# Fused chunk attention and FFN: transposed scores straight into PV, 128-token attention units between FFN steps, q and k loaded in runs of four tokens

## The chip, the cores and the metric

One core of one Trainium2 chip. The time is the device time of one execution in microseconds (us), the median of several runs; lower is better. A profile (a trace of every instruction on every engine) of one execution goes with each kernel. The span in a profile is about 2 us shorter than the timed execution, so I compare spans with spans and times with times. The span of the kernel before, 337.1 us, happens to equal its median time: by the same 2 us its profiled execution took about 339 us (an estimate; that execution is not among the four timed ones).

The engines are named as in the profile: PE is TensorE (matmul), PEld its weight loads, DVE is VectorE, ACT is ScalarE, POOL is GpSimd, which here issues the loads, and SP issues the stores.

## The reference

```python
# attention: q, k, v are (8 batches, 8 heads, 576 tokens, 64), cut into chunks of 64 tokens
scores = 1/sqrt(64) * q_c @ k_c.T        # 64 x 64 per chunk and head
attn   = softmax(scores)
out    = attn @ v_c
# heads side by side: x is (4608 tokens, 512); FFN:
a = x @ w1;  b = x @ w2                  # 512 -> 1024
y = ((a * b) @ w3) @ w_out               # 1024 -> 1024 -> 512
```

Both kernels compute w3 @ w_out once ("the w3 product", 1024 x 512), work in bf16, and run the FFN on nine tiles of 512 tokens: per tile 64 matmuls for a and b and 32 for the output, each with 512 columns. An attention chunk is 64 x 64 x 64: the profile lists its score matmuls as 64\*64 with 64 columns, those of the FFN as 128\*128 with 512.

## The kernel before

Per batch and pair of heads, it transposes q and k on TensorE, computes scores with the query on the partitions, normalises on VectorE, transposes the attention weights on TensorE, and multiplies them with v (this product is called PV). Two FFN steps are let through after each head pair.

```python
for hp in range(NHP):                                   # pairs of heads
    for c in range(NCH):                                # 9 chunks
        nc.tensor.transpose(qT_ps[:, c, :], q_bs[:, c, h0*D:(h0+2)*D], ident64)
        nc.tensor.transpose(kT_ps[:, c, :], k_bs[:, c, h0*D:(h0+2)*D], ident64b)
    nc.scalar.copy(qT[:], qT_ps[:]);  nc.scalar.copy(kT[:], kT_ps[:])
    ...                                                 # scores: lhsT = qT, rhs = kT
    nc.scalar.activation(attn_unn[...], sc_ps[...], Exp, scale=scale, bias=0.0)
    nc.vector.reduce_sum(ssum[:], attn_unn[:], axis=X)
    nc.vector.reciprocal(srec[:, :, 0], ssum[:, :, 0])
    nc.vector.tensor_mul(attn_n[:], attn_unn[:], srec.to_broadcast([P, NCH, CHUNK]))
    ...
        nc.tensor.transpose(aT_ps[:, cc, :], attn_n[:, c0 + cc, :], ident)
    nc.vector.tensor_copy(attnT[...], aT_ps[...])
    ...                                                 # PV: lhsT = v, rhs = attnT
    nc.vector.tensor_copy(xt[:, hp, ...], vo_ps[...])
    pump_moe(PUMP_RATE)
```

(cut: the loads, the w3 product, the FFN steps). All loads go through one queue; q and k come as rows of one token and head.

The softmax here doesn't subtract the row's maximum and nothing guards it: scores larger than these inputs give would overflow.

## Time and profile before

The time is 337.1 us (median of 4 runs, 336.4 to 340.9).

| reading | value | view |
|---|---|---|
| span | 337.1 us | page |
| PE busy | 303.4 us, 90% | page |
| DVE, ACT busy | 165.6, 130.3 us | page |
| one batch of 576 tokens in the steady part | 31.75 us, that is 7.06 us per 128 tokens | chain of waits |
| steady part without any attention | 5.18 us per 128 tokens (24 matmuls of 512 columns at 216 ns) | timeline |

The page of the kernel before: the busy line, and two rows of the span cut into 40 slices of 8.4 us (busy share in tenths; PEclk is the granted TensorE clock in tenths):

```profile
PE 303.4 (90%) x3008; PEld 147.7 (44%) x3008; DVE 165.6 (49%) x360; ACT 130.3 (39%) x245; POOL 111.9 (33%) x146
...
PE   1317999889999999999999999999999999999995
...
PEclk9999999759999999999999999999999999999999
```

PE is nearly idle for three slices, and in the eighth and ninth slices the clock is down. After that everything looks full. Busy time by stretch, for the stretch after the start (columns: busy us and count for PE, PEld, DVE, ACT, POOL, then clock, DMA share, GB/s):

```profile
core 0: us, PE busy (x) PEld busy (x) DVE busy (x) ACT busy (x) POOL busy (x), PEclk, DMA share, GB/s
80.80:333.20 252.40, 248.59 (x2487) 117.34 (x2485) 136.05 (x260) 108.19 (x205) 61.44 (x77) 1.00 0.64 71
```

Of 252.4 us, PE is busy 248.6: the steady part is bound by PE's own work. From 80 to 290 us PE waited for another engine 2.3 us in all (us in total, times, longest):

```profile
PE vo_ps L226 <- DVE attnT L218: 2.3, 11, 0.2
```

The chain of waits (start us, length us, what) shows the wait at the start and one period of the steady part:

```profile
9.25 18.12 DMA tile_bf<-in_moe_w_out_dram
...
184.40 1.40 PE o_ps L125 x6
186.86 0.77 DVE ssum L206
187.90 0.77 DVE attn_n L210
...
216.15 1.40 PE o_ps L125 x6
```

The 18.1 us are the load of w_out, on which the w3 product waits. The same o_ps step recurs after 31.75 us. The row sum and the product of the softmax, 0.77 us each, stand in the chain one after the other.

The groups that the change touches (line, engine, operation, tile written and read, shapes, count; busy us and mean ns; idle time before them and who ended it):

```profile
L216 PE MATMUL aT_ps<-ident,attn_n 128*64 128x128 bf16 x288 | 29.4, 230 | 4.4 <-DVE attn_n L210 2.9
L187 ACT COPY qT<-qT_ps 128x576 bf16<-128x576 bf16 x32 | 20.5, 639 | 21.3 <-PE kT_ps L184 17.6
...
L226 PE MATMUL vo_ps<-attnT,v_bs 64*64 64x64 bf16 x576 | 21.5, 199 | 3.6 <-DVE attnT L218 3.6
```

### The profile page before, as it was taken

To read this page: it belongs to the slowest core of one execution; us is meant where nothing else is said; L and a number is where in the kernel's file an instruction comes from. 1 tells how busy PE (TensorE), PEld (TensorE's weight loads), DVE (VectorE), ACT (ScalarE), POOL (GpSimd) and SP (SyncE) were. 2 spreads that over 40 slices of the span, in tenths; PEclk is the share of its full clock that TensorE was granted. 3 is DMA by queue.
4 is the path that set the end of the run, shared out by engine and by line. 5 is a ranking of instruction groups with operands and counts; after the bars stand their busy time and mean duration, and the time that the engine had idled before them with its cause. 6 is when DMAs were issued, how large, how long until landed. Compare 5 with 4: busy or idle time off the path is not lost.

```text
span 337.1 us, 7133 instructions
## 1 busy us (share of the span) xinstructions
PE 303.4 (90%) x3008; PEld 147.7 (44%) x3008; DVE 165.6 (49%) x360; ACT 130.3 (39%) x245; POOL 111.9 (33%) x146
## 2 busy tenths in 40 slices
PE   1317999889999999999999999999999999999995
PEld 0203455554444444444444444444444444444442
DVE  0211346565756555664556465566555664541330
ACT  2201323433334445345543544444445345333332
POOL 8707259848202009502930491078000000000000
PEclk9999999759999999999999999999999999999999
DMA  9999999949729009942990599099902001101103
GB/s 61 163 203 143 207 155 110 135 27 151 50 93 101 4 31 158 122 31 71 155 112 2 90 166 84 2 138 128 73 31 95 2 2 62 64 3 62 62 0 126
DMA packets 121119, 29.30 MB, mean 87 GB/s; under 512 B 113408, under 2 KB 114432, under 8 KB 121088
## 3 DMA queue, kind: packets, MB, share of 16 engines
q0 software_dynamic: 115904, 19.41, 75.0%
q1 hardware_dynamic: 5184, 9.44, 7.5%
q8 instruction: 24, 0.39, 0.5%
q14 instruction: 7, 0.06, 0.1%
HBM read 38.80 MB, written 9.44 MB: 143 GB/s over the span
## 4 chain that ended last, share of the span: by engine, by line
PE 68%; DVE 14%; DMA 5%; ACT 5%; issue 3%; POOL 2%; POOLq 0%; ACTq 0%
PE b_ps L110 16%; PE a_ps L103 15%; PE o_ps L125 11%; PE aT_ps L216 8%; DMA tile_bf<-in_moe_w_out_dram 5%; PE wp L83 5%; PE vo_ps L226 5%; DVE attn_n L210 5%; DVE ssum L206 5%; PE sc_ps L199 3%; ACT attn_unn L202 3%; DVE attnT L218 2%; PE qT_ps L183 2%; PE tp L79 2%; DVE abT L118 1%
## 5 line engine op out<-in xcount | busy, mean ns | idle before, releaser
L103 PE MATMUL a_ps<-xt,tile_bf 128*128 128x512 bf16 x288 | 82.5, 388 | 0.0
L110 PE MATMUL b_ps<-xt,tile_bf 128*128 128x512 bf16 x288 | 81.7, 386 | 0.0
L166 POOL DMA_DIRECT2D qk_bs<-in_q_dram x64 | 51.3, 802 | 82.9 <-PE kT_ps L184 76.6
L117 ACT COPY a_sb<-a_ps 128x512 f32<-128x512 f32 x72 | 42.3, 588 | 84.7 <-PE a_ps L103 84.7
L125 PE MATMUL o_ps<-w3out_sb,abT 128*128 128x512 bf16 x288 | 68.7, 380 | 0.0
L118 DVE TENSOR_TENSOR abT<-a_sb,b_ps 128x512 bf16<-128x512 f32 x72 | 49.2, 683 | 37.3 <-PE b_ps L110 36.4
L168 POOL DMA_DIRECT2D qk_bs<-in_k_dram x64 | 51.3, 802 | 15.0 <-DMA tile_bf<-in_moe_w_dram 11.9
L206 DVE TENSOR_REDUCE ssum<-attn_unn 128x9 f32<-128x576 bf16 x32 | 24.1, 754 | 51.8 <-ACT attn_unn L202 51.8
L228 DVE CAST xt<-vo_ps 128x320 bf16<-128x320 f32 x64 | 29.3, 458 | 30.9 <-PE vo_ps L226 30.0
L103 PEld LDWEIGHTS <-tile_bf 128*128 128x128 bf16 x288 | 26.7, 99 | 28.7 <-issue 1.9
L110 PEld LDWEIGHTS <-tile_bf 128*128 128x128 bf16 x288 | 26.6, 99 | 27.2 <-issue 1.6
L125 PEld LDWEIGHTS <-abT 128*128 128x128 bf16 x288 | 25.2, 98 | 27.5
L202 ACT ACTIVATE attn_unn<-sc_ps 128x320 bf16<-128x320 f32 x64 | 24.7, 410 | 27.8 <-PE sc_ps L199 23.0
L218 DVE COPY attnT<-aT_ps 64x640 bf16<-64x640 bf16 x64 | 28.5, 445 | 11.4 <-PE aT_ps L216 11.2
L132 ACT COPY o_sb<-o_ps 128x512 f32<-128x512 f32 x36 | 21.1, 586 | 31.9 <-PE o_ps L125 31.9
L216 PE MATMUL aT_ps<-ident,attn_n 128*64 128x128 bf16 x288 | 29.4, 230 | 4.4 <-DVE attn_n L210 2.9
L187 ACT COPY qT<-qT_ps 128x576 bf16<-128x576 bf16 x32 | 20.5, 639 | 21.3 <-PE kT_ps L184 17.6
L216 PEld LDWEIGHTS <-attn_n 128*64 128x64 bf16 x288 | 18.4, 112 | 17.4 <-DVE attn_n L210 15.3
L226 PEld LDWEIGHTS <-v_bs 64*64 64x64 bf16 x576 | 14.7, 109 | 25.1 <-issue 16.8
L80 DVE COPY w3Tk<-tp 128x128 bf16<-128x128 bf16 x64 | 11.0, 219 | 28.4 <-PE tp L79 27.6
L226 PE MATMUL vo_ps<-attnT,v_bs 64*64 64x64 bf16 x576 | 21.5, 199 | 3.6 <-DVE attnT L218 3.6
L210 DVE TENSOR_TENSOR attn_n<-attn_unn,srec 128x576 bf16<-128x576 bf16 x32 | 24.3, 758 | 1.1
(23 smaller groups left out, 185.0 us busy)
## 6 DMA issues: line engine op xcount, KB each, us to landing
out_dram<-o_sb SPq DMA_DIRECT2D x36, 256.0 KB, 2.0
qk_bs<-in_q_dram POOLq DMA_DIRECT2D x64, 72.0 KB, 3.9
qk_bs<-in_k_dram POOLq DMA_DIRECT2D x64, 72.0 KB, 3.8
v_bs<-in_v_dram POOLq DMA_DIRECT2D x8, 576.0 KB, 7.6
tile_bf<-in_moe_w_dram POOLq DMA_DIRECT2D x1, 2048.0 KB, 13.7
tile_bf<-in_moe_w_dram POOLq DMA_DIRECT2D x2, 1024.0 KB, 13.4
tile_bf<-in_moe_w_out_dram POOLq DMA_DIRECT2D x1, 1024.0 KB, 18.1
```

The source lines that it names most:

```text
L103: nc.tensor.matmul(a_ps[:], lhsT=w1_sb[:, ki, j * P:(j + 1) * P], rhs=x_slice[:, ki, :], start=(ki == 0), stop=(ki == D_MO - 1),)
L110: nc.tensor.matmul(b_ps[:], lhsT=w2_sb[:, ki, j * P:(j + 1) * P], rhs=x_slice[:, ki, :], start=(ki == 0), stop=(ki == D_MO - 1),)
L117: nc.scalar.copy(a_sb[:], a_ps[:])
L118: nc.vector.tensor_mul(abT[:, j, :], a_sb[:], b_ps[:])
L125: nc.tensor.matmul(o_ps[:], lhsT=abT[:, ki, tk * P:(tk + 1) * P], rhs=w3out_sb[:, ki, :], start=(ki == 0), stop=(ki == D_FO - 1),)
L166: nc.gpsimd.dma_start(q_bs[:, :, h * D:(h + 1) * D], q[b, h].rearrange("(c p) d -> p c d", p=CHUNK))
L168: nc.gpsimd.dma_start(k_bs[:, :, h * D:(h + 1) * D], k[b, h].rearrange("(c p) d -> p c d", p=CHUNK))
L206: nc.vector.reduce_sum(ssum[:], attn_unn[:], axis=mybir.AxisListType.X)
L210: nc.vector.tensor_mul(attn_n[:], attn_unn[:], srec.to_broadcast([P, NCH, CHUNK]))
L216: nc.tensor.transpose(aT_ps[:, cc, :], attn_n[:, c0 + cc, :], ident)
L218: nc.vector.tensor_copy(attnT[:, :nc_, :], aT_ps[:, :nc_, :])
L226: nc.tensor.matmul(vo_ps[ph:ph + CHUNK, cc, :], v_bs[:, j, :], attnT[:, cc, ph:ph + CHUNK], start=True, stop=True)
```

## The change

The intent is to take work off PE, DVE and ACT in the attention and to feed PE in one planned order.

- Scores are computed transposed (key on the partitions), so exp's result is directly the stationary operand of PV: no transpose of the weights. The row sum comes from a column of ones next to v, and division happens after PV.
- The unit of work is 128 tokens with all 8 heads, slotted at fixed places between FFN steps; TensorE keeps the order in which the program was written.
- q and k are loaded in runs of four tokens, so that a descriptor carries four rows of 64. Token 4s+r of a group then lies on partition s in run r, so each transpose yields tokens of one r, and k and the exponentials have to be put back in token order when they are copied out of PSUM.
- w1 and w2 are loaded before w_out and w3.

The core of the diff (cut: renamed constants, the FFN steps, which stay the same, and most of the schedule):

```diff
-            nc.scalar.copy(qT[:], qT_ps[:])
-            nc.scalar.copy(kT[:], kT_ps[:])
+        qp = ps.tile([P, NHP, GCH, RUN, SUB], bf, tag="tr", bufs=2, name="qp")
+        kp = ps.tile([P, NHP, GCH, RUN, SUB], bf, tag="tr", bufs=2, name="kp")
+        for hp in range(NHP):
+            for r in range(RUN):
+                for hh in range(2):
+                    for dst, p0 in ((qp, 0), (kp, CH)):
+                        tr(dst[hh * CH:(hh + 1) * CH, hp, :, r, :],
+                           qk[p0:p0 + GP, hp + hh * NHP, g, r * D:(r + 1) * D],
+                           ident[p0:p0 + GP, p0:p0 + GP])
+        nc.vector.tensor_copy(qT_t[b][:, g].rearrange("p n c t -> p (n c t)"),
+                              qp[:].rearrange("p n c r s -> p (n c r s)"))
+        nc.vector.tensor_copy(
+            kT_t[b][:, g].rearrange("p n c (s r) -> p (n c) r s", r=RUN),
+            kp[:].rearrange("p n c r s -> p (n c) r s"))
...
-            nc.vector.reduce_sum(ssum[:], attn_unn[:], axis=mybir.AxisListType.X)
-            nc.vector.tensor_mul(attn_n[:], attn_unn[:], srec.to_broadcast(...))
-                    nc.tensor.transpose(aT_ps[:, cc, :], attn_n[:, c0 + cc, :], ident)
+        nc.scalar.activation(
+            e[:].rearrange("p n c (s r) -> p (n c) r s", r=RUN),
+            sp[:].rearrange("p n c (r s) -> p (n c) r s", r=RUN),
+            Exp, scale=scale, bias=0.0)
...
+                    mm(xp[ci * CH:(ci + 1) * CH, hh, hp * W:(hp + 1) * W],
+                       lhsT=e[h, hp, ci, :], rhs=v_t[b][h, hp, c, 0:W],   # W = 65
+                       start=True, stop=True)
+        nc.vector.reciprocal(rc[:], xv[:, :, :, D:D + 1])
+        nc.vector.tensor_mul(xn[...], xv[:, :, :, 0:D], rc.to_broadcast(...))
+            tr(tp[:, hp, :], xn[:, hp], ident[:])
+        nc.vector.tensor_copy(xt[:, :, u * UT:(u + 1) * UT], tp[:])
...
+    for i, f in enumerate(fill):         # fill: the FFN steps in order
+        if i in slots:
+            u = slots[i]
+            if u == UPT:                 # the first unit after the start
+                run_T(groups_for(u + 1))
+                do_S(u)
+            slot_a(u)                    # q,k transposes ahead, scores u+1, PV u
+            pending = u
+        f()                              # one FFN step
+        if pending is not None:
+            do_XT(pending)               # output transposes of u
+            pending = None
```

## The prediction

Its sum comes to 284 us.

> **What bounds the kernel now.** TensorE, in two parts. From 80.8 to 333.2 us (busy time by stretch) it is busy 248.6 of 252.4 us at clock 1.00, and waits for another engine only 2.3 us (the waits). A 512-column FFN matmul is issued every 216 ns (timeline), so a 512-token FFN tile costs 96 x 0.216 = 20.7 us, nine tiles 187 us, the w3·w_out product about 17.6 us. One batch of 576 tokens repeats every 31.75 us (chain, 184.40 to 216.15); 23.3 us of it is FFN, so attention costs 8.4 us per batch, 67 us in all. These sum to 272 us. The other 65 us are mostly before 81 us: TensorE is mostly idle to 27 us, waiting for w3 and w_out (chain: 18.1 us on w_out), then attention's vector chain (sum, reciprocal, product, 1.9 us) leaves gaps, and from 64 to 77 us the granted clock is 0.50. [...]
>
> **What changes, with durations from this trace.** Spacings: q/k transposes one pair per 29 ns (two row groups side by side), scores 15 to 16 ns each, PV 27 ns (one row group), a 128-column transpose about 68 ns; a change between 64-wide and 128-wide use about 0.1 us (first qT step 0.13 us, then 0.03)[...].
> - Removed: 288 attention transposes (20 us), their evictions, row sum (24.1 us) and product (24.3 us) on VectorE, q/k evictions on ScalarE (41 us; VectorE takes them).
> - PV alternates row groups: about 16 ns x 576, saves 6 us.
> - Added: q/k transposes 576 to 1536 with 48 columns, about 12 ns each: 8.5 to 18 us; 144 output transposes, 9 us.
> - Per 128-token unit: transposes 0.55, scores 0.26, PV 0.28, output transposes 0.24, mode changes 0.23: 1.55 us against 1.87. For 32 units inside the FFN 50 us against 60.
> - VectorE per unit 3.8 us of 7, ScalarE 2.4: no limit. The output transpose waits one FFN step (1.73 us) for q/k copies, reciprocal and product (2 to 2.4 us): up to 0.4 us stall in some units.
> - DMA: q,k descriptors carry four times as much; w1,w2 come before w_out,w3, so FFN tile 0 starts while w3 lands. At the rates here (150 to 200 GB/s in slices 2 to 6) batch 0 is there at 14 us, the first halves of w1,w2 at 20, w3 at 43, batch 1's q,k at 48 to 50. The in-order PE needs batch 1 inside the w3 product, near 46 us: a 2 to 5 us gap.
>
> **Sum.** FFN start 20 + FFN 187 + w3 product 17.6 + units 50 + gap and slow clock at the start 5 + tail 4 (333.3 to 337.1 here) = 284 us. Of the gain about 40 of 53 us is the start-up, 10 the steady state.
>
> **What would show it.** First FFN matmul near 20 us; TensorE dense from there, with one gap near 46 to 50 us on batch 1's loads; a tile period of 26.5 to 27.5 us; 64 q/k transposes in 0.7 to 1 us; PV at 16 ns; clock 0.5 only before 40 us; VectorE near 45%; packets about half.
>
> **What would make it wrong.** Transposes into strided 16-element runs issued at 25 ns or more (+20 us); [...] stalls at each output transpose turning the clock down; a throttle. Or the transposes overlap in four quadrants and the stalls vanish (-10 us).

## The result

The changed kernel takes 309.1 us (median of 4 runs, 307.5 to 311.2) and is correct. Its ratio to the kernel before is 0.915 (95% interval 0.909 to 0.922). Ratios here are the mean time of one kernel's fast runs over that of the other's of the same rounds, so they are not quite the ratios of the medians that I quote. So it is 8% faster, but 25 us slower than predicted.

The page after:

```profile
PE 258.6 (84%) x3824; PEld 132.4 (43%) x3824; DVE 149.7 (49%) x239; ACT 110.8 (36%) x153; POOL 43.2 (14%) x55
...
PE   1244999679888888988988889889889889999994
...
PEclk9999999959999999999999999999999999999999
```

The start is shorter, but the row that was full of nines is now a pattern of eights and nines. The stretch of FFN tiles with attention between them, after:

```profile
core 0: us, PE busy (x) PEld busy (x) DVE busy (x) ACT busy (x) POOL busy (x), PEclk, DMA share, GB/s
88.17:282.00 193.83, 178.26 (x2657) 88.80 (x2657) 106.41 (x174) 79.32 (x112) 15.82 (x16) 1.00 0.59 72
```

PE is busy 178 of 194 us: it waits here, which it did not before. The groups that answer to those shown of before (tiles: qp and kp hold the q and k transposes in PSUM, qT and kT their copies, sp the scores, e the exponentials, xp the result of PV, xn that result divided by the row sum, tp the output transposes):

```profile
L155 ACT ACTIVATE e<-sp 128x512 bf16<-128x512 f32 x36 | 47.0, 1306 | 36.2 <-PE sp L66 32.3
...
L133 DVE COPY kT<-kp 128x768 bf16<-128x768 bf16 x24 | 44.2, 1842 | 0.0
...
L130 DVE COPY qT<-qp 128x768 bf16<-128x768 bf16 x24 | 13.4, 557 | 41.8 <-PE kp L69 41.8
L69 PE MATMUL tp<-ident,xn 128*128 128x128 bf16 x144 | 15.0, 230 | 21.7 <-DVE xn L177 21.7
```

Two copies of the same size, 128 x 768 bf16 out of PSUM, both on DVE: q takes 557 ns, k 1842 ns. And the output transposes (tp) waited 21.7 us on the vector product xn, 15.6 us of it from 88 to 282 us, where the view lists no other wait of PE:

```profile
PE tp L69 <- DVE xn L177: 15.6, 16, 1.0
```

The chain of waits shows how the two are connected:

```profile
201.19 0.14 PE qp L69
...
201.89 0.55 DVE qT L130
202.44 1.76 DVE kT L133
...
204.26 0.70 DVE xn L177
...
205.00 0.40 PE tp L69 x4
...
208.85 0.31 PE sp L66 x12
...
214.86 0.14 PE qp L69
...
222.52 0.14 PE qp L69
```

At 201.19 the unit's q,k transposes begin, and from 201.89 the chain is on DVE: q copy, k copy, reciprocal, product, until the output transposes at 205.00. In the program the copies of the next group stand in front of the product xn on DVE, and the trace runs them in this order (k copy from 202.44, product from 204.26), although the product does not need them. Meanwhile PE ran one FFN step and then had nothing it was allowed to do. The units begin at 201.19 (with q,k transposes), 208.85 (without), 214.86 and 222.52: 7.66, 6.01, 7.66 us. Three of them take 21.33 us, or 7.11 us per 128 tokens. It was 7.06 before. **The steady part did not become faster at all**; the whole gain of 28 us is in the start.

The start after, from the chain:

```profile
6.14 8.18 DMA qk<-in_k_dram
...
16.02 1.76 DVE kT L133
...
24.71 1.76 DVE kT L133
...
31.56 1.86 PE a_ps L66 x4
...
88.17 0.97 PE a_ps L66 x4
```

The second third of batch 0's q,k lands at 14.3 us, about when the prediction had the whole batch. PE waited for no load between 14.4 us and the first FFN matmul; the four units before the FFN run one after another, and PE waited 9.6 us for VectorE there (4.6 for k copies, 4.2 for the products xn, 0.8 for copies of x). So the first FFN matmul is at 31.56 us, not at 20. FFN tile 1 begins at 88.17. And in between the clock falls to half, as these windows show:

```profile
56.00:60.00 4.00, 1.71 (x115) 1.18 (x114) 2.30 (x2) 0.61 (x2) 0.00 (x0) 1.00 1.69 184
60.00:64.00 4.00, 1.80 (x123) 1.56 (x113) 2.30 (x2) 1.27 (x1) 0.00 (x0) 0.66 0.71 69
64.00:68.00 4.00, 4.00 (x51) 2.33 (x44) 3.45 (x5) 1.31 (x1) 3.62 (x4) 0.50 0.50 61
```

This is where three groups of q,k transposes follow each other with only one unit's scores between them. The scores waited 2.3 us for the first group's k copy; the other groups, each of which needs both PSUM buffers, waited 0.6 and 1.6 us for the copies of the group before. PE is busy 1.7 and 1.8 of 4 us, then works at clock 0.50. The longest wait of PE in this stretch was 2.3 us. In the kernel before the clock fell near 64 us, with PE busy 2.82 of 4 us from 60 to 64 us and no wait longer than 1.0 us. What turns the clock down was not shown: no run here separates the share of busy time from the kind of work.

### The profile page after: what moved, and what is told of

Same layout as the page of the kernel before. It is cut to its first block, busy times and chain, and to the rows that moved or that the text cites. A ratio compares the mean times of both kernels' runs of the same rounds, so it can differ in the third digit from the quotient of the medians.

```text
span 307.0 us, 8414 instructions
## 1 busy us (share of the span) xinstructions
PE 258.6 (84%) x3824; PEld 132.4 (43%) x3824; DVE 149.7 (49%) x239; ACT 110.8 (36%) x153; POOL 43.2 (14%) x55
## 2 busy tenths in 40 slices
DMA packets 65395, 29.37 MB, mean 96 GB/s; under 512 B 38224, under 2 KB 59728, under 8 KB 65360
## 4 chain that ended last, share of the span: by engine, by line
PE 70%; DVE 23%; DMA 3%; POOL 1%; issue 1%; ACT 0%; DVEq 0%; ACTq 0%; POOLq 0%
PE o_ps L66 19%; PE a_ps L66 16%; PE b_ps L66 16%; DVE kT L133 13%; DVE xn L177 5%; PE wp L66 5%; PE tp L69 4%; DVE qT L130 4%; PE qp L69 3%; DMA qk<-in_k_dram 3%; PE sp L66 2%; PE kp L69 2%; PE xp L66 1%; PE w3tp L69 1%; DVE ab L203 1%
## 5 line engine op out<-in xcount | busy, mean ns | idle before, releaser
L203 DVE TENSOR_TENSOR ab<-a_sb,b_ps 128x512 bf16<-128x512 f32 x72 | 49.3, 685 | 69.6 <-PE b_ps L66 69.6
L66 PE MATMUL a_ps<-xt,w_77 128*128 128x512 bf16 x288 | 75.0, 383 | 0.5 <-DVE xt L186 0.5
L66 PE MATMUL b_ps<-xt,w_78 128*128 128x512 bf16 x288 | 74.3, 380 | 0.0
L202 ACT COPY a_sb<-a_ps 128x512 f32<-128x512 f32 x72 | 44.2, 613 | 73.5 <-PE a_ps L66 70.2
L66 PE MATMUL o_ps<-w3o,ab 128*128 128x512 bf16 x288 | 67.4, 379 | 0.0
L155 ACT ACTIVATE e<-sp 128x512 bf16<-128x512 f32 x36 | 47.0, 1306 | 36.2 <-PE sp L66 32.3
L133 DVE COPY kT<-kp 128x768 bf16<-128x768 bf16 x24 | 44.2, 1842 | 0.0
L66 PEld LDWEIGHTS <-w_78 128*128 128x128 bf16 x288 | 28.4, 98 | 34.5 <-issue 1.1
L66 PEld LDWEIGHTS <-ab 128*128 128x128 bf16 x288 | 27.9, 98 | 33.1
L66 PEld LDWEIGHTS <-w_77 128*128 128x128 bf16 x288 | 24.9, 98 | 22.7 <-issue 1.2
L69 PE MATMUL tp<-ident,xn 128*128 128x128 bf16 x144 | 15.0, 230 | 21.7 <-DVE xn L177 21.7
L69 PE MATMUL qp<-ident,qk 48*64 48x48 bf16 x768 | 19.1, 194 | 9.0 <-DMA qk<-in_q_dram 8.3
L177 DVE TENSOR_TENSOR xn<-xp,rc 128x512 bf16<-128x512 f32 x36 | 24.9, 691 | 1.6
## 6 DMA issues: line engine op xcount, KB each, us to landing
vbuf_83<-in_v_dram POOLq DMA_DIRECT2D x6, 288.0 KB, 6.8
vbuf_84<-in_v_dram POOLq DMA_DIRECT2D x6, 288.0 KB, 12.8
vbuf_85<-in_v_dram POOLq DMA_DIRECT2D x4, 288.0 KB, 16.5
```

The source lines that it names most:

```text
L66: return inorder(nc.tensor.matmul(*a, **kw))
L69: return inorder(nc.tensor.transpose(*a, **kw))
L133: nc.vector.tensor_copy(kT_t[b][:, g].rearrange("p n c (s r) -> p (n c) r s", r=RUN), kp[:].rearrange("p n c r s -> p (n c) r s"))
L155: nc.scalar.activation(e[:].rearrange("p n c (s r) -> p (n c) r s", r=RUN), sp[:].rearrange("p n c (r s) -> p (n c) r s", r=RUN), Exp, sca ...
L177: nc.vector.tensor_mul(xn[:].rearrange("p n t d -> p t n d"), xv[:, :, :, 0:D], rc.to_broadcast([P, 2, NHP, D]))
L202: nc.scalar.copy(a_sb[:], a_ps[:])
```

## The experiments

The main theory, A: the copy that puts k back in token order is slow because its two-byte elements are written 8 bytes apart; it sits in front of the softmax product on DVE and so in front of the output transposes on PE. Rivals: B, the lost time is the start-up's load order and its serial head; C, the exponentials, which are scattered in the same way (1.31 us each), hold up PV or the FFN's evictions (copies out of PSUM) on ACT; D, DVE lacks throughput. The head, below, is the part of the kernel before its first FFN matmul.

All times are medians of fast runs, but for the two single runs, whose state is unknown; one slow run of the kernel before was left out of the ratios. In each set the kernel before took 336.8 to 337.3 us (median).

| run | what | result | us | ratio to before (95%) |
|---|---|---|---|---|
| (changed kernel) | | right | 309.1 | 0.915 (0.909 to 0.922) |
| k_plain_wrong | k copied in PSUM's order | wrong | 284.4 | 0.845 (0.839 to 0.852) |
| k_read_strided | the shuffle on the read side | right | 291.9 | 0.866 (0.860 to 0.873) |
| xt_late | output transposes one step later | right | 293.0 | 0.870 (0.865 to 0.875) |
| exp_plain_wrong | exp in PSUM's order | rows permuted | 309.4 | 0.918 (0.912 to 0.924) |
| head_reorder | start-up overlapped | right | 305.0 | 0.904 (0.900 to 0.908) |
| read_late | k_read_strided and xt_late | right | 289.6 | 0.859 (0.855 to 0.863) |
| v_perm | no k shuffle, v permuted by its loads | right | 288.0 | 0.854 (0.850 to 0.858) |
| best1 | read_late, head_reorder, earlier batch 1 | right | 285.6 | 0.848 (0.843 to 0.853) |
| best2 | best1, transposes spread | right | 285.0 | 0.843 (0.838 to 0.849) |
| best3 | best1 with v_perm for k_read_strided | right | 289.8 | 0.860 (0.854 to 0.866) |
| k_write_4b | writes 4 bytes apart | wrong | 293.0 (one run) | |
| k_write_32b | writes 32 bytes apart | wrong | 365.1 (one run) | |

### Without the shuffle (k_plain_wrong)

```diff
-            kT_t[b][:, g].rearrange("p n c (s r) -> p (n c) r s", r=RUN),
-            kp[:].rearrange("p n c r s -> p (n c) r s"))
+            kT_t[b][:, g].rearrange("p n c t -> p (n c t)"),
+            kp[:].rearrange("p n c r s -> p (n c r s)"))
```

> Wrong result on purpose: k is evicted in the order PSUM has it, with nothing else changed. Theory A (the strided k eviction, 1.84 us against 0.56 us for q's of the same size, delays the output transposes and the head): the k copy falls to about 0.56 us, the waits of the output transposes on the vector product fall from 21.7 us to under 3 us, the clock dip near 62 to 67 us shrinks, the time falls to 278 to 284 us. Theory B (the lost time is the start-up's DMA order and the serial head): the time falls by less than 8 us.

Measured: 284.4 us, 24.7 us less, just above the band that A gave. The groups of this run:

```profile
L69 PE MATMUL tp<-ident,xn 128*128 128x128 bf16 x144 | 14.8, 229 | 4.2 <-DVE xn L176 4.2
...
L133 DVE COPY kT<-kp 128x768 bf16<-128x768 bf16 x24 | 13.1, 547 | 0.0
```

The k copy fell from 1842 to 547 ns, and the waits of the output transposes from 21.7 to 4.2 us, all of them in the head (A had expected under 3 us). The clock was down in one window of 4 us (0.57 from 60 to 64 us) where it had been down in two (0.66 and 0.50). One edit to one copy is worth 24.7 us, with the same PE instructions, so A holds and B cannot be the main cause. D is not excluded yet, since the edit also takes 31 us of work off DVE (44.2 to 13.1); xt_late, below, tests it. Where the 24.7 us went: the first FFN matmul is at 27.94 us (was 31.56: 3.6 us), the way from there to tile 1, at 81.71 us, is 53.8 us (was 56.6: 2.8 us), and from tile 1 to the end of the span of 282.3 us it is 200.6 us (was 218.8: 18.2 us).

One unit in its chain of waits:

```profile
194.93 0.14 PE qp L69
...
195.56 0.18 PE sp L66 x11
...
195.81 0.13 PE xp L66 x10
195.94 0.97 PE a_ps L66 x4
...
197.78 0.22 PE tp L69 x4
```

The q,k transposes begin at 194.93 and the scores' own part of the chain at 195.56, so 64 transposes took 0.63 us; the last ten PV matmuls add 0.13 us; at 195.94 the FFN goes on, and at 197.78 the output transposes follow without a gap. Three units take 19.05 us (this unit with transposes begins at 194.93, and the third after it at 213.98), or 6.35 us per 128 tokens.

### Shuffle on the read side (k_read_strided)

```diff
-            kT_t[b][:, g].rearrange("p n c (s r) -> p (n c) r s", r=RUN),
-            kp[:].rearrange("p n c r s -> p (n c) r s"))
+            kT_t[b][:, g].rearrange("p n c (s r) -> p (n c) s r", r=RUN),
+            kp[:].rearrange("p n c r s -> p (n c) s r"))
```

> Right result: the same permutation, but the copy walks so that writes to SBUF are contiguous and reads from PSUM are strided. If it is the scattered two-byte writes that cost, the k copy takes 0.6 to 0.95 us and the time is 280 to 288 us. If it is the permutation itself (short inner runs, here even shorter, 4 elements), the copy stays at 1.8 us or more and the time at 305 us or more.

Measured: 291.9 us, right result. The same permutation, walked in the order of the destination:

```profile
L133 DVE COPY kT<-kp 128x768 bf16<-128x768 bf16 x24 | 22.7, 947 | 0.0
...
L69 PE MATMUL tp<-ident,xn 128*128 128x128 bf16 x144 | 15.0, 230 | 7.2 <-DVE xn L177 7.2
```

947 instead of 1842 ns, although its inner runs are shorter (4 against 16). So it is not the permutation that costs, but the scattered writes. The time lies 4 us above the band I wrote; a wait of 7.2 us at the output transposes is left, 4.2 us of it in the head as in k_plain_wrong, and the rest because the chain on DVE (0.56 + 0.95 + 0.20 + 0.69 us) is still a little longer than what PE has to do meanwhile.

The step from 547 to 947 ns is (947 - 547) / 768 = 0.52 ns per element; the one from 947 to 1842, with the scattered writes, is another 1.17. Why the strided read or the scattered writes cost this much was not shown.

### How far apart (k_write_4b, k_write_32b)

```diff
-            kT_t[b][:, g].rearrange("p n c (s r) -> p (n c) r s", r=RUN),
-            kp[:].rearrange("p n c r s -> p (n c) r s"))
+            kT_t[b][:, g].rearrange("p n c (s r) -> p (n c) r s", r=X),     # X = 2, 16
+            kp[:].rearrange("p n c a t -> p (n c) (a t)").rearrange("p m (r s) -> p m r s", r=X))
```

> Wrong result on purpose: the k eviction reads PSUM contiguously and writes to SBUF with a stride of 4 bytes instead of 8 (runs of 32). If a scattered write costs by how many of its elements share a short stretch of SBUF, the copy takes clearly less than the 1.84 us at 8 bytes (0.9 to 1.4). If any scattered write costs the same, 1.8 us.

> Wrong result on purpose: the same with a stride of 32 bytes (runs of 4). By the first idea the copy takes 1.84 us or more; if short strides are the bad ones, less.

Measured, the k copies of the two kernels:

```profile
L133 DVE COPY kT<-kp 128x768 bf16<-128x768 bf16 x24 | 23.9, 998 | 0.0
```

```profile
L133 DVE COPY kT<-kp 128x768 bf16<-128x768 bf16 x24 | 81.3, 3387 | 0.0
...
L69 PE MATMUL tp<-ident,xn 128*128 128x128 bf16 x144 | 16.3, 245 | 49.3 <-DVE xn L177 49.2
```

The copy takes 547 ns with contiguous writes, 998 with writes 4 bytes apart, 1842 at 8 and 3387 at 32. The cost rises with the distance of successive writes. The inner runs get shorter along with it (32, 16 and 4 elements), but short runs alone are not the cost: k_read_strided had runs of 4 and took 947 ns. The whole kernel follows: at 32 bytes the output transposes wait 49.3 us and the time is 365 us, at 4 bytes 293 us. These are single runs, but the effects are many times their spread. The direction is that of the first idea; why the cost rises so was not shown. At 8 bytes apart the copy already takes twice the time of the one that is strided on the read side (1842 against 947 ns).

### Later output transposes (xt_late)

```diff
-        if pending is not None:
+        if pending is not None and (i not in slots or i < first + 2 * UPT):
             do_XT(pending)
```

> The strided copy stays at 1.84 us, but the output transposes of the units inside tiles 1 to 8 come one FFN step (1.73 us) later. If the copy hurts there as latency that the in-order TensorE waits out (A), the waits of the output transposes fall from 21.7 us to about 4 us and the time to 289 to 293 us. If VectorE were short of throughput, or the copies' own work the limit, the time stays above 303 us.

Measured: 293.0 us, at the edge of what A expected, and right.

```profile
L133 DVE COPY kT<-kp 128x768 bf16<-128x768 bf16 x24 | 44.2, 1843 | 0.0
...
L69 PE MATMUL tp<-ident,xn 128*128 128x128 bf16 x144 | 14.8, 229 | 6.1 <-DVE xn L177 6.1
```

The copy is as slow as ever, but the transposes now wait 6.1 us instead of 21.7. Three units take 19.05 us here too (191.16 to 210.21 us in its chain), exactly as without the shuffle. So inside the FFN the slow copy cost nothing but latency on the path of the in-order PE: D falls. What is left of the difference to k_plain_wrong (8.6 us) lies in the part before tile 1, which begins at 87.08 us here and at 81.71 there (5.4 us), and in the FFN part, where three times, 2.5 us in all, q,k transposes now waited for the copy of the later output transposes out of the PSUM buffer that they share.

### Exp in PSUM's order (exp_plain_wrong)

```diff
-            e[:].rearrange("p n c (s r) -> p (n c) r s", r=RUN),
-            sp[:].rearrange("p n c (r s) -> p (n c) r s", r=RUN),
+            e[:].rearrange("p n c t -> p (n c t)"),
+            sp[:].rearrange("p n c t -> p (n c t)"),
```

> Wrong result on purpose: exp writes in the order PSUM has it. Exp, 1.31 us now, falls to about 0.6 us. Theory A: exp is finished long before its unit's PV inside the FFN, so only the head gains: 305 to 308 us. Rival C (ScalarE's scattered exp holds up PV or the FFN's evictions): 300 us or less.

Measured: 309.4 us, no change.

```profile
L155 ACT ACTIVATE e<-sp 128x512 bf16<-128x512 f32 x36 | 21.6, 599 | 37.7 <-PE sp L66 33.2 <-PE xp L66 4.4
```

Exp went from 1306 to 599 ns, 25 us of ACT work, and the time did not move; not even the 1 to 4 us that I expected of the head. C falls. The contrast teaches the most here: the same kind of scattering, at a similar cost per element ((1306 - 599) / 512 = 1.4 ns on ACT, (1842 - 547) / 768 = 1.7 ns on DVE), is worth 25 us on DVE and nothing on ACT. (The comparison with the reference passed this kernel although it permutes the rows inside each chunk. Probably the scores of this input are so small that the rows of one chunk's result are nearly equal; I did not check this.)

### The start-up (head_reorder)

Batch 0's q,k go ahead of its v, and the four units before the FFN are interleaved.

```diff
-    load_v(0)
     load_qk(0, 1, 2)
     load_qk(0, 2, 3)
+    load_v(0)
...
-    for u in range(UPT - 1):
-        run_T(groups_for(u + 1)); do_S(u + 1); do_PV(u); do_XT(u)
-    do_PV(UPT - 1); do_XT(UPT - 1)
+    run_T(2); do_S(1); run_T(3); do_PV(0); do_S(2); do_PV(1); do_XT(0)
+    do_S(3); do_PV(2); do_XT(1); do_PV(3); do_XT(2); do_XT(3)
```

> Right result, strided k eviction kept. Batch 0's q,k are loaded ahead of its v, and the four units before the FFN are overlapped instead of taken one by one. If the prediction's start (FFN at 20 us, it was 31.6) failed because of load order and the serial head, the first FFN matmul moves to 20 to 24 us; the time falls by 4 to 10 us (299 to 305) unless the later loads (w3, batch 1) take the gain back, in which case it stays at 306 to 309 and TensorE waits on DMA between 35 and 55 us.

Measured: 305.0 us, 4.1 us less. The first FFN matmul in its timeline:

```profile
26.00 1.86 PE L66 MATMUL a_ps<-xt,w 128*128 128x512 bf16 x4 [0.52 <-DVE xt L186]
```

It moved from 31.56 to 26.00 us, not to the 20 to 24 that would have borne out the prediction's start. B is real but small.

### Both cures, and the way without any shuffle (read_late, v_perm)

read_late joins the edits of k_read_strided and xt_late. v_perm copies k as it lies, and permutes v's rows to match, by loading v in pieces of 16 partitions:

```diff
-            load(v_t[b][hh * CH:(hh + 1) * CH, :, :, 0:D].rearrange("p n c d -> p (n c) d"),
-                 v[b, hh * NHP:(hh + 1) * NHP].rearrange("n (c p) d -> p (n c) d", p=CH))
+            for r in range(RUN):
+                p0 = hh * CH + r * SUB
+                load(v_t[b][p0:p0 + SUB, :, :, 0:D].rearrange("p n c d -> p (n c) d"),
+                     v[b, hh * NHP:(hh + 1) * NHP]
+                     .rearrange("n (c s r) d -> r s (n c) d", s=SUB, r=RUN)[r])
```

> Right result: strided PSUM reads for k (0.95 us) and output transposes one FFN step later, together. The two cures act on the same waits, so they must not add up: from 291.9 and 293.0 alone to 283 to 287 together, with waits of output transposes under 4 us.

> Right result without any strided k copy: k is evicted as it lies (0.55 us) and v is loaded in the matching row order, in 16-partition pieces. If the wrong-result run priced the shuffle rightly, 282 to 287 us like it (284.4); if the 16-partition loads cost, the head is longer and the time 287 to 295 us.

Measured: read_late 289.6 us. Alone the two cures saved 17.3 and 16.1 us, together 19.5: they act on the same waits, as A says. The waits of the output transposes are 4.5 us and the time is 2.6 us above the band. v_perm: 288.0 us, with k copies of 547 ns, and the first FFN matmul at 29.6 us instead of the 27.9 of k_plain_wrong: the loads in small pieces took back some of the gain, as the second branch had it.

### Putting it together (best1, best2, best3)

best1 joins k_read_strided, xt_late and head_reorder, and loads batch 1's q,k ahead of w_out and w3. best2 loads batch 0's v ahead of its last third of q,k, and, the point of it, the three groups of batch 1 that stood back to back come one each in steps 5, 6 and 7 of FFN tile 0.

```diff
+    def ab0(j):
+        if j >= 5:
+            run_T(j - 1)
+        do_ab(0, j)
```

best3 is best1 with v_perm's loads and plain k copy.

> Right result: strided PSUM reads, later output transposes, overlapped head, and batch 1's q,k loaded ahead of w_out and w3. Theory: the steady part is as in read_late (6.3 to 6.4 us a unit) and the FFN starts at 19 to 22 us, so 270 to 278 us. If w3's later arrival stalls TensorE instead, 279 to 285 us with DMA waits before 60 us.

> Right result. As best1, but batch 1's three q,k transpose groups come one each in steps 5, 6 and 7 of FFN tile 0 instead of back to back inside the w3 product, and batch 0's v is loaded ahead of its last third of q,k. If the back-to-back groups (each holds both PSUM buffers until its copies end) made the gap and the half clock at 51 to 60 us in best1, the gap and the dip go and the time falls by 5 to 8 us to 277 to 281. If that gap was DMA, the time stays at 283 to 287.

> Right result: best1 (285.6 us) with v_perm's loads in place of the strided PSUM reads, so that no copy is strided (k 0.55 us instead of 0.95). In the FFN part the transposes no longer wait in either, so only the head can gain: 282 to 285 us. If the sixteen-partition loads delay the head as they did in v_perm (FFN start 29.6 against 27.9 us), 285 to 288 us.

Measured: best1 285.6 us, best2 285.0, best3 289.8. All three missed their first branch, and best1 and best3 lie above their second one too. best1 gained 4 us on read_late; its FFN starts at 25.7 us instead of 28.4. In best2 the dip of the clock at 56 to 60 us (0.60 in best1) did go and the gap shrank (PE busy 2.5 of 4 us from 52 to 56, 1.4 in best1), as its windows show (the clock is third from the right):

```profile
52.00:56.00 4.00, 2.50 (x56) 1.39 (x54) 0.67 (x1) 1.90 (x3) 0.00 (x0) 1.00 2.06 174
56.00:60.00 4.00, 4.00 (x43) 2.43 (x35) 2.61 (x5) 1.89 (x2) 2.29 (x2) 1.00 1.64 190
60.00:64.00 4.00, 4.00 (x58) 2.27 (x57) 1.68 (x4) 2.21 (x3) 0.00 (x0) 1.00 1.80 173
...
72.00:76.00 4.00, 2.74 (x37) 1.27 (x38) 1.65 (x3) 1.30 (x1) 0.00 (x0) 0.76 0.41 104
```

but a gap of 2 us and a dip of the clock (0.76 in the last window) came up around 72 us instead. So the gain was given back later. The profile names no releaser for that wait ("issue"), and I did not find its cause. In best3 the output transposes waited only 1.1 us in all, yet it lost 4 us to best1. POOL was busy issuing the small pieces of v (4.0 and 3.4 of 4 us between 52 and 60 us), and PE waited 2.1 us for a load of w3, which best1 did not; I did not separate these.

## Why the prediction was wrong

What the prediction had right: faster by a margin; PE binds and DVE and ACT have throughput to spare (DVE 49%, predicted 45%); 64 q,k transposes in 0.7 us; packets about half (121119 to 65395); the output transpose as the place where a wait would stand; the wait named as a risk (the clock, which it was to turn down, stayed at 1.00 from 88 to 282 us). The spacing of the transposes into 16-element runs, the first risk in the text, turned out harmless (0.63 us for 64 of them).

What failed, step by step:

1. **"The output transpose waits one FFN step (1.73 us) for q/k copies, reciprocal and product (2 to 2.4 us): up to 0.4 us stall in some units."** The mechanism is right, but the k copy is mis-sized. Two copies at the rate of q's are 1.1 us; k's alone took 1.84 us, because it writes two-byte elements 8 bytes apart. The chain on DVE is 0.56 + 1.84 + 0.20 + 0.69 = 3.3 us, and the wait about 1 us in two of three units (16 waits, 15.6 us, from 88 to 282 us; none there in k_plain_wrong). The sum of the prediction had no term for this wait. The experiments price the slow copy at 24.7 us: 18.2 from tile 1 on, where this wait stands, and 6.4 before it. That is also why the 10 us that the steady state was to gain did not come (7.11 us per 128 tokens against 7.06 before). I took a duration from a copy of the same size and ignored that its access pattern was another.
2. **"FFN start 20", and dense from there.** It was 31.6 us. Batch 0's loads were not what failed: after 14.4 us PE waited for none of them. What the prediction left out is the serial chain of the four units, 17.2 us from there, 9.6 of it waits for VectorE. A plain k copy alone takes 3.6 us off this start (k_plain_wrong), the order of loads and units alone 5.6 (head_reorder); they do not simply add, since best1, with that order and the 947 ns copy, starts its FFN at 25.7 against the 26.0 of head_reorder. By the sum of the prediction, tile 1 should begin at about 71 us (284, less eight tiles at 20.7, 28 units at 1.55 and the tail of 4); in k_plain_wrong, where the copy no longer disturbs, it begins at 81.7. So the start was 11 us too short by itself, 8 of it before the first FFN matmul (27.9 against 20) and 3 after. Reordering recovered 4 us of time. The rest is not settled: the first FFN matmuls at half speed (1.86 us for four, 0.86 later, while the granted clock reads 1.00) and the second gap in the w3 product stand in the traces, but no run separates them.
3. **"Units 50."** Too dear. 6.35 us less 5.18 is 1.17 us per unit, not 1.55. The 64 transposes cost 0.63 us, about 10 ns each, in place of about 0.83 (0.55 per unit, 36 units, 24 groups), and scores and PV run partly beside them and beside each other: this fits the four-quadrant overlap (in the changed kernel's timeline four transposes begin at 201.20 to 201.21 us, the next four at 201.23 to 201.24), which I had put among the things that could make the prediction wrong (-10 us). From tile 1 to the end the prediction allowed 213 us; without the shuffle it took 200.6, with it 218.8.

So k_plain_wrong lands on the predicted 284 us partly by luck: 11 us too little for the start and 12 too much for the units cancel. The miss of the kernel itself is one mis-sized copy, worth 24.7 us, on top.

The change of mode between small and full matmuls was sized rightly: the first four FFN matmuls after the small ones take 0.97 us in the chain instead of 0.86, and the first transpose 0.14 us, about 0.1 us each way.

## What to carry to other kernels

Price a copy by how its writes lie, not by its size: when data must be permuted on the way out of PSUM, walk in the order of the destination and put the stride on the read side (0.95 us here against 1.84), or permute something that is loaded anyway. When a tensor engine that keeps program order is slotted with work for another engine, sum up the whole in-order queue in front of the one result it needs, including work that this result does not depend on; if it does not fit into the slot, collect the result one slot later. (Issuing the next group's copies behind the product should help as well; no run here tried it.) And a slow instruction is worth what waits for it: the same kind of scattering cost 25 us on one engine and nothing on the other.
